# Batch 0 of a linear-attention and feed-forward kernel: k, v, q loaded in this order as fp32, q taken in pieces of tokens

## The chip, the cores and the metric

The kernel runs on one core of one Trainium2 chip. TensorE (PE) multiplies matrices, VectorE (DVE) and ScalarE (ACT) do elementwise work and read PE's results out of PSUM, GpSimd (POOL) and SyncE (SP) mostly issue DMAs here. Each engine takes its instructions in program order and waits for others by semaphores. The metric is the device time in microseconds. A profile is of one execution, with its span and the names of the engines as above; "PEld" is PE's weight load.

## The reference

```python
def phi(x):
    return np.where(x > 0, x, np.exp(x) - 1.0) + 1.0
q_p, k_p = phi(q), phi(k)                      # q, k, v: (8, 8, 576, 64) fp32
kv  = np.einsum('bhsd,bhse->bhde', k_p, v)
z   = np.sum(k_p, axis=2)
num = np.einsum('bhsd,bhde->bhse', q_p, kv)
den = np.einsum('bhsd,bhd->bhs', q_p, z)[..., None] + 1e-06
x   = (num / den).transpose(0, 2, 1, 3).reshape(8 * 576, 512)
h   = x @ w_in                                 # (512, 2048)
g   = h * (1.0 / (1.0 + np.exp(-beta * h)))
out = g @ w_out                                # (2048, 512)
```

The kernel computes phi as min(exp(x), max(x, 0) + 1), and g as Silu(beta * h) with 1/beta put into w_out.

## The kernel before, in words

A batch has 576 tokens; a token is 9 g + j, with g from 0 to 63 on partitions and j from 0 to 8 in the free dimension (J = 9). Eight heads lie as two "pr" (pairs of pairs), two "i" or "il" and two halves of the partitions, "a" or "hh". Blocks of two j make four token blocks t = 0 to 3 of 128 rows, and j = 8 is a tail block t = 4 of 64 rows, which is kept in xT_tail and multiplied at the very end for all batches together.

A batch goes through: loads of q, k, v; phi (phi_exp on ACT, line 161, phi_relu and phi_min on DVE, lines 166 and 174); transposes of phi(q) on PE; kv and z; numerators and denominators; xs = numerator times 1/denominator (bf16); transposes of xs into xT; h_mm (line 398), the product with w_in, in 16 chunks ff; silu (line 411), ACT's evacuation into g; y_mm (line 416) or y_fast, the product with w_out. The attention part of batch b+1 is put among the y products of batch b. The order is written by hand: the kernel asks for a manual schedule, so the order of the source lines is that of each engine's queue.

The front is lines 106 to 617, batch 0, in which no earlier products lie beside the attention:

- Loads (lines 106 to 138). SyncE's queue takes q in two halves of heads (x0f[0], x0f[1]) and k in two (x0f[2], x0f[3]), all fp32, into the buffer "stage" and the memory of xk[0]. POOL's queue waits by a small copy, "gate" (line 123), for q's first half and then issues v in two halves, cast to bf16 by the DMA (v0b, in vf's memory), w_in in four quarters (cast as well), w_out's first two quarters in fp32 (into the memory of g of batch 1), and q and k of batch 1 (cast). load_w_out(2) and load_w_out(3) go into stage, load_v(1) into vf as fp32; these and load_qk(2) are issued at lines 620 to 623.
- PE begins with 11 products on made-up data (idle, line 151), and more of them fill waits.
- phi of q's first half, its transposes (q_half, line 243), the same for the second half, q_last for the tail; phi of k's halves.
- z is computed by itself (z_sums, 18 products of one column per half), kv_first (line 511) makes kv from 128-column products that hold two heads and their cross terms, kv_mask and zbd remove the cross terms by a mask on DVE. All denominators come from 20 products into one bank, dps, and denom (line 557).
- numer_first(t) (line 565) makes the numerators of block t on PE and xs on DVE; x_first(t) transposes them and copies to xT; h_first(t) makes 16 products of 128 columns, the part of h chunks ff = 0 to 3 that belongs to block t. silu of these four banks needs all four blocks. Chunks 4 to 15 follow as 512-column products.

Y0, lines 632 to 698, holds batch 0's y products with batch 1's attention among them: y_mm(0, t, i) adds w_out's quarter i to token block t, four products of 512 columns each; kv_both(1) (line 213) uses vaug, v of batch 1 with a column of ones, which ACT and POOL cast from vf (lines 650 and 651). w_out_scale (line 449) makes w_out's quarters from their fp32 loads. The pool of PSUM banks for kv, numerators and x transposes has two buffers there (line 619).

Of the kernel before, what the change touches and what calls it, by code (L numbers as in the profile page):

```python
# [16 lines left out]
def kernel(  # L17
# [65 lines left out]
    x3f = xk[0].rearrange("p i j d -> p (i j d)").bitcast(F32)  # L83
    x0f = [
        a.rearrange("p (i j d) -> p i j d", i=2, j=J)
        for a in [stage[:, n * 1152 : (n + 1) * 1152] for n in range(3)] + [x3f]
    ]
# [52 lines left out]
    kvmask = consts.tile([P, 2, 2, EA], BF16)  # L140
    nc.vector.memset(kvmask, 0.0)
    nc.vector.memset(kvmask[:D, :, 0, :], 1.0)
    nc.vector.memset(kvmask[D:P, :, 1, :], 1.0)
    ones = consts.tile([P, 1], BF16)
    nc.vector.memset(ones, 1.0)
# [333 lines left out]
    qtp = [bank1("qtp", [P, 1024], BF16) for _ in range(2)]  # L479
    phi_part(0, "q", 0)  # L480
    q_half(0, 0, qtp[0])
    idle(3)
    phi_part(0, "q", 1)
    q_half(0, 1, qtp[1])
    t8 = bank1("qtp8", [P, 2 * P], BF16)
    q_last(0, t8)
    bps = bank("bps", [P, FC])
    nc.tensor.matmul(bps, beta_row, ident16, is_transpose=True, start=True, stop=True)
    idle(4)
    x = xin(0, "k", 0)  # L490
    phi_exp(0, "k", 0, x)
    phi_relu(0, "k", 0, x)
    q_copy(nc.vector, 0, 0, qtp[0])
    phi_min(0, "k", 0)


    zps = [bank("zps") for _ in range(2)]
    zbd = consts.tile([P, 2, 2, 2], BF16)

    def z_sums(pr):  # L500
        for j in range(J):
            for hh in range(2):
                nc.tensor.matmul(
                    zps[hh][:, pr : pr + 1], st[0, "k"][half(hh), pr, j, :], ones[half(hh)],
                    start=(j == 0), stop=(j == J - 1), skip_group_check=True,
                )

    kvp0 = [bank1("kvp0") for _ in range(2)]
    kv0 = consts.tile([P, 2, 2, 2 * D], BF16)

    def kv_first(pr):
        for j in range(J):
            for hh in range(2):
                nc.tensor.matmul(
                    kvp0[hh][:, pr * P : (pr + 1) * P],
                    st[0, "k"][half(hh), pr, j, :],
                    v0b[half(hh), 2 * pr : 2 * pr + 2, j, :],
                    start=(j == 0), stop=(j == J - 1), skip_group_check=True,
                )

    def kv_mask(pr):
        for hh in range(2):
            nc.vector.tensor_mul(
                kv0[:, hh, pr].rearrange("p (h d) -> p h d", h=2),
                kvp0[hh][:, pr * P : (pr + 1) * P].rearrange("p (h d) -> p h d", h=2),
                kvmask[:, hh, :, 0:D],
            )

    z_sums(0)
    idle(1)  # L530
    phi_part(0, "k", 1)
    q_copy(nc.scalar, 0, 1, qtp[1])
    q_copy_last(nc.scalar, 0, t8)
    nc.scalar.copy(beta_s, bps)
    table(ACTF.Silu)
    kv_first(0)
    z_sums(1)
    idle(1)
    kv_mask(0)
    for hh in range(2):  # L540
        nc.vector.tensor_mul(
            zbd[:, hh], zps[hh][:, 0:2, None].to_broadcast([P, 2, 2]), kvmask[:, :, :, 0]
        )
# [11 lines left out]
    dv = dps.rearrange("p t a b c -> p t (a b c)")

    def denom(r, ts):
        nc.vector.tensor_scalar(den0[:r, ts], dv[:r, ts], 1e-6, None, ALU.add)
        nc.vector.reciprocal(rden0[:r, ts], den0[:r, ts])

    kv_first(1)
    denom(P, slice(0, NT - 1))
    kv_mask(1)

    def numer_first(t):
        n = rows_of(t)
        nps = bank1("nps0", [P, 2, 2, P])
        for hh in range(2):
            for pr in range(2):
                nc.tensor.matmul(  # L570
                    nps[:n, hh, pr], st[0, "qT"][:, pr, t, hh, 0:n], kv0[:, hh, pr, :],
                    start=True, stop=True, skip_group_check=True,
                )
        nc.vector.tensor_mul(
            xs_tile(0, t),
            nps[:n].rearrange("p a b (c d) -> p a (b c) d", d=D),
            rden0[:n, t].rearrange("p (a i) -> p a i", a=2)[:, :, :, None].to_broadcast(
                [n, 2, 4, D]
            ),
        )  # L580

    def x_first(t, eng):
        x_trans(0, t, eng, bank1("xtp0", [P, KC, P], BF16))


    hp0 = []

# [15 lines left out]
    h_first(1)
    x_first(3, nc.scalar)
    nc.vector.tensor_mul(beta_m, beta_s, beta_s)
    nc.vector.tensor_scalar(beta_m, beta_m, TINY * TINY, 2.0 * TINY, ALU.is_lt, ALU.mult)
    nc.vector.tensor_add(beta_c, beta_s, beta_m)
    nc.vector.reciprocal(rbeta, beta_c)
    h_first(2)
# [303 lines left out]
```

## Time and profile before

| | |
|---|---|
| Median of 3 runs | 278.42 us (278.10 to 278.65) |
| The profiled execution | 277.78 us, span 276.0 us |
| PE busy | 267.8 us (97% of the span) |
| DVE, ACT busy | 169.7 us (61%), 170.1 us (62%) |
| DMA moved | 42.76 MB, mean 155 GB/s |
| First h product of batch 0 | 16.67 us after the span's start |
| Last of the four h_first starts | 20.55 us |
| First h product of batch 1 | 51.09 us |

The profile's times are counted from the span's start. Lines of the timeline give start, duration, engine, source line, operation, output <- inputs, shapes and count; in brackets stands the idle time before and what ended it. A helper's line stands for all its callers (L404 is every h product). Busy time by stretch gives, for PE, PEld, DVE, ACT and POOL, the busy us and the count, then PE's granted clock, the DMA share and the GB/s moved.

### The profile page before, as it was taken

What the parts mean: (1) busy time and instruction counts of PE and PEld (TensorE: products, weight loads), DVE (VectorE), ACT (ScalarE), POOL (GpSimd) and SP (SyncE); (2) the same over time, 40 slices, a digit from 0 to 9 for tenths busy, and PEclk for the clock granted to TensorE, in tenths of its full rate; (3) what the DMA queues carried; (4) which work ended last, traced back from release to release, by engine and by line L of the source; (5) the groups of instructions that cost most, each with busy time, mean ns of one, the idle gap of its engine ahead of it and who ended that gap; (6) DMA issues with size and microseconds to landing.
All of it is one profiled execution on the core that took longest, in us unless ns stands there. A gap on an engine that the chain in (4) does not pass through costs nothing.

```text
span 276.0 us, 6367 instructions
## 1 busy us (share of the span) xinstructions
PE 267.8 (97%) x2688; PEld 167.6 (61%) x2697; DVE 169.7 (61%) x329; ACT 170.1 (62%) x232; POOL 45.6 (17%) x60
## 2 busy tenths in 40 slices
PE   7899999999999999999999999999999999999994
PEld 2575455444445487548754885488548845874683
DVE  4771585967956997568857884779473414342532
ACT  4838887966915794579457945794573077117610
POOL 5922011042123040303030403040000000000000
PEclk9999999999999999999999999999999999999999
DMA  6999999569969946996799659956531040022013
GB/s 231 254 206 352 255 387 250 177 109 192 297 109 189 312 65 109 196 289 78 102 201 289 81 89 209 296 79 88 154 66 22 13 141 0 0 68 87 0 40 114
DMA packets 49228, 42.76 MB, mean 155 GB/s; under 512 B 30752, under 2 KB 41008, under 8 KB 49200
## 3 DMA queue, kind: packets, MB, share of 16 engines
q0 software_dynamic: 13040, 23.40, 36.4%
q1 hardware_dynamic: 35984, 18.82, 32.3%
q8 instruction: 21, 0.34, 0.5%
q10 hardware_dynamic: 176, 0.14, 0.2%
q14 instruction: 7, 0.06, 0.1%
HBM read 36.71 MB, written 9.44 MB: 167 GB/s over the span
## 4 chain that ended last, share of the span: by engine, by line
PE 82%; DMA 13%; DVE 1%; POOL 1%; issue 1%; ACT 0%; DVEq 0%; POOLq 0%
PE h_ps L404 41%; PE yb L795 9%; PE ya L795 9%; PE yd L795 9%; DMA vf<-in_v_dram 8%; PE y_ps L419 6%; PE yc L795 4%; DMA w_in<-in_moe_w_in_dram 4%; PE kvp L223 2%; PE nps L331 2%; DMA stage<-in_q_dram 1%; POOL vf L100 1%; PE nps L298 1%; DVE xs_sb L311 1%; ACT vaug L239 0%
## 5 line engine op out<-in xcount | busy, mean ns | idle before, releaser
L412 ACT ACTIVATE g<-h_ps,beta_c 128x512 bf16<-128x512 f32 x144 | 97.8, 688 | 69.1 <-PE h_ps L404 69.1
L404 PE MATMUL h_ps<-xT,w_in 128*128 128x512 bf16 (+1 forms) x560 | 114.5, 361 | 0.1
L404 PEld LDWEIGHTS <-w_in 128*128 128x128 bf16 x624 | 57.4, 98 | 62.3 <-issue 0.2
L795 PEld LDWEIGHTS <-stage 128*128 128x128 bf16 x448 | 43.8, 98 | 5.2
L795 PEld LDWEIGHTS <-g 128*128 128x128 bf16 x336 | 32.9, 98 | 5.3
L241 POOL CAST vaug<-vf 128x1152 bf16<-128x1152 f32 x13 | 18.4, 1443 | 74.7 <-DMA vf<-in_v_dram 74.7
L419 PE MATMUL y_ps<-w_out,g 128*128 128x512 bf16 x122 | 28.4, 379 | 0.4 <-issue 0.2
L795 PE MATMUL ya<-w_out,g 128*128 128x256 bf16 x224 | 26.7, 273 | 0.0
L725 DVE TENSOR_TENSOR stage<-g 128x1024 bf16<-128x1024 bf16 x14 | 9.6, 686 | 22.8 <-ACT g L412 22.8
L729 DVE TENSOR_TENSOR stage<-g 128x1024 bf16<-128x1024 bf16 x14 | 9.7, 691 | 19.2 <-ACT g L412 19.2
L346 DVE TENSOR_TENSOR xs_sb<-nps,rden 128x448 bf16<-128x448 f32 (+3 forms) x30 | 20.7, 689 | 1.0
L419 PEld LDWEIGHTS <-g 128*128 128x128 bf16 x128 | 12.2, 98 | 13.5
L163 ACT ACTIVATE e<-xk 128x1152 bf16<-128x1152 bf16 (+1 forms) x15 | 16.7, 1159 | 0.3 <-DMA xk<-in_k_dram 0.3
L163 ACT ACTIVATE e<-xq 128x1152 bf16<-128x1152 bf16 x14 | 15.6, 1160 | 0.0
L175 DVE TENSOR_TENSOR phi_k<-e,r 128x1152 bf16<-128x1152 bf16 x16 | 13.5, 850 | 1.4
L156 ACT ACT_TABLE_LOAD x11 | 14.1, 1283 | 0.2
L404 PE MATMUL h_ps<-xT_tail,w_in 128*128 128x512 bf16 x62 | 13.9, 379 | 0.1
L795 PE MATMUL yd<-ws,stage 128*128 128x256 bf16 x112 | 13.4, 273 | 0.0
L795 PE MATMUL yb<-ws,stage 128*128 128x256 bf16 x112 | 13.4, 272 | 0.0
L795 PE MATMUL yc<-ws,stage 128*128 128x256 bf16 x112 | 13.4, 273 | 0.0
L795 PE MATMUL yd<-ws,g 128*128 128x256 bf16 x112 | 13.4, 273 | 0.0
L795 PE MATMUL yb<-w_out,stage 128*128 128x256 bf16 x112 | 13.4, 272 | 0.0
(98 smaller groups left out, 233.8 us busy)
## 6 DMA issues: line engine op xcount, KB each, us to landing
vf<-in_v_dram POOLq DMA_DIRECT2D x7, 1152.0 KB, 13.3
out_dram<-y SPq DMA_DIRECT2D x25, 256.0 KB, 3.8
xq<-in_q_dram POOLq DMA_DIRECT2D x7, 576.0 KB, 8.3
xk<-in_k_dram POOLq DMA_DIRECT2D x7, 576.0 KB, 10.9
out_dram<-y SPq DMA_DIRECT2D x17, 128.0 KB, 2.9
w_in<-in_moe_w_in_dram POOLq DMA_DIRECT2D x4, 512.0 KB, 11.8
g<-in_moe_w_out_dram POOLq DMA_DIRECT2D x2, 1024.0 KB, 17.4
stage<-in_moe_w_out_dram POOLq DMA_DIRECT2D x2, 1024.0 KB, 21.6
```

The costliest lines, as they stand in the source:

```text
L156: nc.scalar.activation(act0, warm[:, 0:1], func)
L163: nc.scalar.activation(e, x, ACTF.Exp)
L175: nc.vector.tensor_tensor(st[b, a][:, pr].rearrange("p j (h d) -> p j h d", h=2), st[b, a, pr, "e"].rearrange("p h j d -> p j h d"), st[b, ...
L223: nc.tensor.matmul(t[half(il), a, pr * EA : (pr + 1) * EA], st[b, "k"][half(a), pr, j, il * D : (il + 1) * D], vaug[b % 2][half(a), pr, j, ...
L241: eng.tensor_copy(dst, src)
L346: nc.vector.tensor_mul(xs_sb[:n, ils, v0 * D : v1 * D].rearrange("p i (u d) -> p i u d", d=D), pv[:, :, :, 0:D], rden[:, :, :, None].to_br ...
L404: nc.tensor.matmul(hp[:, c0:c1].rearrange("p (t n) -> p t n", n=P), w_in_sb[ff // 4][:, kc, (ff % 4) * P : (ff % 4 + 1) * P], xm, start=(k ...
L412: nc.scalar.activation(g_sb[b % 2][:, ff, :], hp, ACTF.Silu, scale=beta_c[:, ff : ff + 1])
L419: nc.tensor.matmul(yp[:, c0:c1], g_sb[b % 2][:, ff, t * P : (t + 1) * P], w_out_sb[i][:, c, c0:c1], start=(ff == 0), stop=(ff == FC - 1), ...
L725: nc.vector.tensor_sub(gs[2][:, c], g[:, c, 0:HM], g[:, c, HM:512])
L729: nc.vector.tensor_add(gs[0][:, c], g[:, c, HM:512], g[:, c2, HM:512])
L795: nc.tensor.matmul(ps[:, p * HM : (p + 1) * HM], lhs(c, p), rhs(c), start=(first and (p == 0 or apart) and c == 0), stop=True, skip_group_ ...
```

## The change

Batch 0's loads on SyncE's queue become k in two halves, v in two halves (fp32, into vf) and q in two pieces of tokens: all heads with j = 0 to 3 (four j, blocks 0 and 1), then j = 4 to 8. POOL's gate waits for k's second half, and its queue no longer loads v. v is cast on chip into vaug, the first half by ACT, the second by DVE (v_copy). kv and the sums of phi(k) come from the same products by vaug's column of ones, in 64x65 products as in kv_both; kv_out copies them from PSUM into kv_bd, two copies per pr and half, and the mask, the ones and z_sums are gone. phi of q is done by pieces (class Part): j 0-1 and j 2-3 for all heads, then j 4-8 for each pr. q_first(t) transposes one block. Blocks 0 and 1 go through denominator, numerator, xs, x transposes and h_first before blocks 2, 3 and 4 are transposed. beta's sums are moved ahead on DVE. load_w_out(3) becomes two DMAs of half the size, and in Y0 kv_both(1) stands one y_mm later, with numer(1, 0) and numer(1, 1) directly behind each other.

```diff
-    load(nc.sync, x0f[0], q, 0, 0, 2)
-    load(nc.sync, x0f[1], q, 0, 2, 2)
-    load(nc.sync, x0f[2], k, 0, 0, 2)
-    load(nc.sync, x0f[3], k, 0, 2, 2)
+    for pr in range(2):
+        load(nc.sync, x0k[pr], k, 0, 2 * pr, 2)
+    for pr in range(2):
+        load(nc.sync, vf[:, 2 * pr : 2 * pr + 2], v, 0, 2 * pr, 2)
+    load(nc.sync, x0q[0], q, 0, 0, 4, 0, 4)
+    load(nc.sync, x0q[1], q, 0, 0, 4, 4, 5)
...
-    nc.gpsimd.tensor_copy(gate, x0f[0][:, 1, J - 1, D - 1 : D])
-    load(nc.gpsimd, v0b[:, 0:2], v, 0, 0, 2)
-    load(nc.gpsimd, v0b[:, 2:4], v, 0, 2, 2)
+    nc.gpsimd.tensor_copy(gate, x0k[1][:, 1, J - 1, D - 1 : D])
...
+    bps = bank("bps", [P, FC])
+    nc.tensor.matmul(bps, beta_row, ident16, is_transpose=True, start=True, stop=True)
+    idle(6)
...
+    for pr in range(2):
+        phi_part(0, "k", pr)
+    nc.vector.tensor_copy(beta_s, bps)
+    nc.vector.tensor_mul(beta_m, beta_s, beta_s)
+    nc.vector.tensor_scalar(beta_m, beta_m, TINY * TINY, 2.0 * TINY, ALU.is_lt, ALU.mult)
+    nc.vector.tensor_add(beta_c, beta_s, beta_m)
+    nc.vector.reciprocal(rbeta, beta_c)
...
     def kv_first(pr):
         for j in range(J):
+            for il in range(2):
+                for a in range(2):
+                    nc.tensor.matmul(
+                        kvp0[a][half(il), pr * EA : (pr + 1) * EA],
+                        st[0, "k"][half(a), pr, j, il * D : (il + 1) * D],
+                        vaug[0][half(a), pr, j, il, 0:EA],
+                        start=(j == 0), stop=(j == J - 1), skip_group_check=True,
+                    )
+
+    def kv_out(pr, a, eng):
+        for il in range(2):
+            copy(
+                eng, kv_bd[half(il), a, pr, il], kvp0[a][half(il), pr * EA : (pr + 1) * EA]
+            )
+
+    class Part:
...
+        def exp(self):
+            nc.scalar.activation(self.e, self.x, ACTF.Exp)
+
+        def relu(self):
+            nc.vector.tensor_scalar(self.r, self.x, 0.0, 1.0, ALU.max, ALU.add)
+
+        def min(self):
+            for i in range(0, self.n, 2):
+                nc.vector.tensor_tensor(
...
+    def q_first(t, eng):
+        tp = bank1("qtp", [P, 512], BF16)
+        for pr in range(2):
+            for jj in range(2):
                 nc.tensor.matmul(
+                    tp.rearrange("p (r h i g) -> p r h i g", r=2, h=2, i=2)[:, pr, :, jj, :],
+                    st[0, "q"][:, pr, 2 * t + jj, :], identity,
+                    is_transpose=True, start=True, stop=True, skip_group_check=True,
...
+    v_copy(nc.scalar, 0, 0)
+    kv_first(0)
+    v_copy(nc.vector, 0, 1)
+    for a in range(2):
+        kv_out(0, a, nc.vector)
+    idle(2)
+    kv_first(1)
+    idle(3)
+    qa = [Part(x0q[0][:, :, 2 * n : 2 * n + 2], 0, 2 * n) for n in range(2)]
+    for n in range(2):
+        qa[n].exp()
+        qa[n].relu()
+        if n == 0:
+            qa[0].min()
+    kv_out(1, 0, nc.vector)
+    kv_out(1, 1, nc.scalar)
+    q_first(0, nc.scalar)
+    qa[1].min()
+    den_mm(dps, (0,))
+    numer_mm0(0)
+    denom(dps, P, slice(0, 1))
+    numer_xs0(0)
+    q_first(1, nc.scalar)
+    dps1 = bank("dps", dps_shape)
+    den_mm(dps1, (1,))
+    numer_mm0(1)
+    qb = [Part(x0q[1][:, 2 * pr : 2 * pr + 2], 2 * pr, 4) for pr in range(2)]
+    qb[0].exp()
     x_first(0, nc.scalar)
+    denom(dps1, P, slice(1, 2))
+    numer_xs0(1)
     h_first(0)
+    qb[0].relu()
+    qb[0].min()
+    qb[1].exp()
+    qb[1].relu()
+    table(ACTF.Silu)
+    x_first(1, nc.vector)
+    qb[1].min()
+    h_first(1)
+    q_first(2, nc.scalar)
+    q_first(3, nc.vector)
+    t8 = bank1("qtp8", [P, 2 * P], BF16)
+    q_last(0, t8)
+    q_copy_last(nc.vector, 0, t8)
+    dps = bank1("dps", dps_shape)
+    den_mm(dps, (2, 3, 4))
+    numer_mm0(2)
+    numer_mm0(3)
+    denom(dps, P, slice(2, 4))
+    numer_xs0(2)
+    numer_xs0(3)
+    denom(dps, G, slice(4, 5))
     x_first(2, nc.scalar)
+    h_first(2)
+    numer_mm0(4)
+    numer_xs0(4)
     x_first(3, nc.scalar)
+    h_first(3)
     x_first(4, nc.vector)
...
-    load_w_out(3)
+    load_w_out(3, 2)
...
-    for t in range(2):
+    for t in range(3):
         y_mm(0, t, 2, yps[t])
     kv_both(1)
...
-    y_mm(0, 2, 2, yps[2])
+    y_mm(0, 3, 2, yps[3])
     numer(1, 0)
-    y_mm(0, 3, 2, yps[3])
     numer(1, 1)
+    y_mm(0, 0, 3, yps[0])
     x_trans(1, 0, nc.scalar)
...
-    y_mm(0, 0, 3, yps[0])
     numer(1, 2)
```

numer_mm0(t) makes block t's four numerator products, numer_xs0(t) its xs on DVE, den_mm its four denominator products, denom adds 1e-6 and takes reciprocals.

More of the change, by code (lines that the diff above doesn't have):

```diff
@@ L82 @@
     ]
[L83 to L86, printed above, removed]
-    ]
-    v0b = vf.rearrange("p i j d -> p (i j d)").bitcast(BF16)[:, 0:2304].rearrange(
-        "p (i j d) -> p i j d", i=4, j=J
-    )
+    x0k = [
+        stage[:, n * 1152 : (n + 1) * 1152].rearrange("p (i j d) -> p i j d", i=2, j=J)
+        for n in range(2)
+    ]
+    x0q = [
+        xk[0].rearrange("p i j d -> p (i j d)").bitcast(F32)[:, 0:1024].rearrange(
+            "p (i j d) -> p i j d", i=4, j=4
+        ),
+        stage[:, 2304:3584].rearrange("p (i j d) -> p i j d", i=4, j=5),
+    ]
     st_b = stage.bitcast(BF16)
@@ L96, with load @@
     ws = [consts.tile([P, 8, HM], BF16, name=f"ws{i}") for i in range(4)] if FAST else None
-    def load(eng, dst, src, b, i0=0, n=4):
+    def load(eng, dst, src, b, i0=0, n=4, j0=0, nj=J):
         return eng.dma_start(
             out=dst.rearrange("p i j d -> p i (j d)"),
-            in_=src[b].rearrange("(i a) (g j) d -> (a g) i (j d)", a=2, j=J)[:, i0 : i0 + n],
+            in_=src[b].rearrange("(i a) (g j) d -> (a g) i (j d)", a=2, j=J)[
+                :, i0 : i0 + n, j0 * D : (j0 + nj) * D
+            ],
         )
@@ L130, with load_w_out @@
         nc.gpsimd.dma_start(out=w_in_sb[i], in_=w_in_v[:, :, i * 512 : (i + 1) * 512])
-    def load_w_out(i):
-        nc.gpsimd.dma_start(out=w_out_f[i], in_=w_out_v[:, i * 4 : (i + 1) * 4, :])
+    def load_w_out(i, n=4):
+        for c in range(0, 4, n):
+            nc.gpsimd.dma_start(
+                out=w_out_f[i][:, c : c + n], in_=w_out_v[:, i * 4 + c : i * 4 + c + n, :]
+            )
     load_w_out(0)
@@ L138 @@
     load(nc.gpsimd, xk[1], k, 1)
[L140 to L145, printed above, removed]
     for i in range(2):
@@ L183, in xin @@
         if b == 0:
-            return x0f[pr if a == "q" else 2 + pr]
+            return x0k[pr]
         return (xk if a == "k" else xq)[b % 2][:, 2 * pr : 2 * pr + 2]
@@ L478 @@
     q_tile(0)
[L479 to L506, printed above, removed]
+    for pr in range(2):
+        phi_part(0, "k", pr)
+    nc.vector.tensor_copy(beta_s, bps)
@@ L508 @@
+    nc.vector.tensor_mul(beta_m, beta_s, beta_s)
+    nc.vector.tensor_scalar(beta_m, beta_m, TINY * TINY, 2.0 * TINY, ALU.is_lt, ALU.mult)
+    nc.vector.tensor_add(beta_c, beta_s, beta_m)
+    nc.vector.reciprocal(rbeta, beta_c)
     kvp0 = [bank1("kvp0") for _ in range(2)]
-    kv0 = consts.tile([P, 2, 2, 2 * D], BF16)
     def kv_first(pr):
         for j in range(J):
-            for hh in range(2):
+            for il in range(2):
[6 more added lines that the diff above has]
+                    )
@@ new lines, in kv_out, with __init__ @@
+    def kv_out(pr, a, eng):
+        for il in range(2):
+            copy(
+                eng, kv_bd[half(il), a, pr, il], kvp0[a][half(il), pr * EA : (pr + 1) * EA]
+            )
+    class Part:
+        def __init__(self, x, i0, j0):
+            self.x, self.i0, self.j0 = x, i0, j0
+            self.n, self.nj = x.shape[1], x.shape[2]
+            self.e, self.r = [
+                work.tile([P, 2, J, D], BF16, tag=s, name=s, bufs=4).rearrange(
+                    "p i j d -> p (i j d)"
+                )[:, 0 : self.n * self.nj * D].rearrange("p (i j d) -> p i j d", i=self.n, d=D)
+                for s in ("e", "r")
+            ]
+        def exp(self):
[5 more added lines that the diff above has]
+                nc.vector.tensor_tensor(
+                    st[0, "q"][:, (self.i0 + i) // 2, self.j0 : self.j0 + self.nj].rearrange(
+                        "p j (h d) -> p j h d", h=2
+                    ),
+                    self.e[:, i : i + 2].rearrange("p h j d -> p j h d"),
+                    self.r[:, i : i + 2].rearrange("p h j d -> p j h d"),
+                    ALU.min,
+                )
@@ L514, in kv_first @@
+    def q_first(t, eng):
+        tp = bank1("qtp", [P, 512], BF16)
+        for pr in range(2):
+            for jj in range(2):
                 nc.tensor.matmul(
[L515 to L518, printed above, removed]
-                )
[L521 to L542, printed above, removed]
+                    tp.rearrange("p (r h i g) -> p r h i g", r=2, h=2, i=2)[:, pr, :, jj, :],
+                    st[0, "q"][:, pr, 2 * t + jj, :], identity,
@@ L543, with den_mm @@
+                    is_transpose=True, start=True, stop=True, skip_group_check=True,
+                )
+        copy(
+            eng, st[0, "qT"][:, :, t].rearrange("p r h n -> p r (h n)"),
+            tp.rearrange("p (r x) -> p r x", r=2),
         )
-    dps = bank("dps", [P, NT, 2, 2, 2])
     den0 = consts.tile([P, NT, 8], F32)
     rden0 = consts.tile([P, NT, 8], F32)
-    for t in range(NT):
+    def den_mm(dps, ts):
+        for t in ts:
+            n = rows_of(t)
+            for hh in range(2):
+                for pr in range(2):
+                    nc.tensor.matmul(
+                        dps[:n, t, hh, pr], st[0, "qT"][:, pr, t, hh, 0:n],
+                        kv_bd[:, hh, pr, :, D], start=True, stop=True, skip_group_check=True,
+                    )
@@ L548, with denom, numer_mm0 @@
+    def denom(dps, r, ts):
+        dv = dps.rearrange("p t a b c -> p t (a b c)")
+        nc.vector.tensor_scalar(den0[:r, ts], dv[:r, ts], 1e-6, None, ALU.add)
+        nc.vector.reciprocal(rden0[:r, ts], den0[:r, ts])
+    def numer_mm0(t):
         n = rows_of(t)
+        nps = st[0, "nps", t] = bank1("nps0", [P, 2, 2, P])
         for hh in range(2):
@@ L551, with numer_xs0 @@
                 nc.tensor.matmul(
-                    dps[:n, t, hh, pr], st[0, "qT"][:, pr, t, hh, 0:n], zbd[:, hh, pr, :],
+                    nps[:n, hh, pr].rearrange("p (h d) -> p h d", h=2),
+                    st[0, "qT"][:, pr, t, hh, 0:n], kv_bd[:, hh, pr, :, 0:D],
                     start=True, stop=True, skip_group_check=True,
                 )
[L555 to L565, printed above, removed]
-        n = rows_of(t)
[L567 to L573, printed above, removed]
+    def numer_xs0(t):
+        n = rows_of(t)
         nc.vector.tensor_mul(
             xs_tile(0, t),
-            nps[:n].rearrange("p a b (c d) -> p a (b c) d", d=D),
+            st[0, "nps", t][:n].rearrange("p a b (c d) -> p a (b c) d", d=D),
             rden0[:n, t].rearrange("p (a i) -> p a i", a=2)[:, :, :, None].to_broadcast(
@@ L592, in h_first @@
             h_mm(xT[0], ff, hp0[ff], t * P, (t + 1) * P)
-    for t in range(3):
-        numer_first(t)
-    denom(G, slice(NT - 1, NT))
+    dps_shape = [P, NT, 2, 2, 2]
+    dps = bank("dps", dps_shape)
+    v_copy(nc.scalar, 0, 0)
[26 more added lines that the diff above has]
+    qb[0].exp()
     x_first(0, nc.scalar)
-    numer_first(3)
-    x_first(1, nc.scalar)
+    denom(dps1, P, slice(1, 2))
+    numer_xs0(1)
     h_first(0)
-    numer_first(4)
+    qb[0].relu()
[19 more added lines that the diff above has]
+    denom(dps, G, slice(4, 5))
     x_first(2, nc.scalar)
-    h_first(1)
+    h_first(2)
+    numer_mm0(4)
+    numer_xs0(4)
     x_first(3, nc.scalar)
[L605 to L609, printed above, removed]
+    h_first(3)
     x_first(4, nc.vector)
-    h_first(3)
     for ff in range(4):
```

## The prediction

> **What bounds the kernel now.** I read the page first, then the chain of waits, then the timeline of the first 21 us, the busy time by microsecond, and the waits. The page and the chain:
>
> ```profile
> span 276.0 us, 6367 instructions
> PE 267.8 (97%) x2688; PEld 167.6 (61%) x2697; DVE 169.7 (61%) x329; ACT 170.1 (62%) x232; POOL 45.6 (17%) x60
> PE 82%; DMA 13%; DVE 1%; POOL 1%; issue 1%; ACT 0%; DVEq 0%; POOLq 0%
> ```
>
> TensorE (PE) is the bound. From the first product of batch 0 to the end it hardly rests, so a change in the front counts in full by the time at which that stream starts, unless the stream later waits for something else and returns the time. The timeline shows the start:
>
> ```profile
> 4.45 1.16 ACT L163 ACTIVATE e<-stage 128x1152 bf16<-128x1152 f32 x1 [1.74 <-DMA stage<-in_q_dram]
> 9.58 1.16 ACT L163 ACTIVATE e<-xk 128x1152 bf16<-128x1152 f32 x1 [0.28 <-DMA xk<-in_k_dram]
> 11.34 0.68 PE L514 MATMUL kvp<-vf,phi_k 64*128 64x128 bf16 x18 [0.65 <-DMA vf<-in_v_dram]
> 14.85 1.29 DVE L574 TENSOR_TENSOR xs_sb<-nps,rden 128x512 bf16<-128x512 f32 x2 [0.31 <-PE nps L570]
> 16.67 1.05 PE L404 MATMUL h_ps<-xT,w_in 128*128 128x128 bf16 x16
> 18.23 1.06 PE L404 MATMUL h_ps<-xT,w_in 128*128 128x128 bf16 x16
> 18.43 0.59 ACT L239 COPY xT<-xtp 128x512 bf16<-128x512 bf16 x1 [1.21 <-PE xtp L386]
> 19.35 1.06 PE L404 MATMUL h_ps<-xT,w_in 128*128 128x128 bf16 x16
> 20.55 11.43 PE L404 MATMUL h_ps<-xT,w_in 128*128 128x128 bf16 x64
> ```
>
> The four x16 or x64 rows are h_first(0) to h_first(3). They start at 16.67, 18.23, 19.35 and 20.55, and all of xT is there by the last, after which PE goes on without a gap. It can go so closely because every phi, q transpose and denominator was done before: when v's second half is in (kv_first(1) at 13.35), only numerators, evacuations and transposes are left, and VectorE (DVE) makes one xs every 0.65 us.
>
> The second place is Y0, where the next batch's v is awaited:
>
> ```profile
> 40.62 1.15 ACT L239 CAST vaug<-vf 128x1152 bf16<-128x1152 f32 x1 [1.06 <-DMA vf<-in_v_dram]
> 41.83 0.80 PE L223 MATMUL kvp<-vaug,phi_k 64*64 64x65 bf16 x72 [0.21 <-ACT vaug L239]
> 49.55 0.23 PEld L386 LDWEIGHTS <-xs_sb 128*128 128x128 bf16 x4 [0.63 <-DVE xs_sb L311]
> ```
>
> PE's idle time from 40 to 50 us, by microsecond, is 0.03, 0.23, 0.16, 0.09, 0, 0.13, 0, 0.03, 0, 0.19: 0.86 us, about 0.25 of it the wait for v. That is all that the Y0 half of the change can win. The DMA rate while SyncE's queue alone moves fp32:
>
> ```profile
> 3.00:4.00 1.00, 1.00 (x4) 0.31 (x3) 0.00 (x0) 0.00 (x0) 0.00 (x0) 1.00 1.03 399
> 4.00:5.00 1.00, 1.00 (x4) 0.45 (x3) 0.55 (x1) 0.55 (x1) 0.52 (x1) 1.00 1.07 401
> 13.00:14.00 1.00, 1.00 (x32) 0.86 (x29) 0.51 (x2) 0.50 (x2) 0.75 (x1) 1.00 1.24 208
> ```
>
> The last column is GB/s written: 400 for fp32, 208 where the load casts (two bytes read for one written). So bytes read go at some 400 GB/s either way, and casting v on chip changes nothing in the total.
>
> **Landings.** A 590 KB piece takes 1.47 us at 400 GB/s. SyncE's four pieces were used at 4.45, 6.37, 8.13 and 9.58; these places now hold k, k, v, v. POOL's gate waits for the second landing, not the first, so its first load (now w_in) is issued at about 6.8 to 7.2 (landing plus 0.78 for the gate), against 5.19 for v and 6.74 for w_in before. Without v's cast load beside them, places 2 to 4 land at 5.9, 7.4 and 8.9 at the earliest and as before at the latest; I take 5.95, 7.4, 9.2. The q pieces (524 and 655 KB, 1.31 and 1.64 us alone) land at 10.2 and 11.8 if w_in leaves them alone, at 12.2 and 14.5 if it halves their rate from 9 us on. I take 10.9 and 13.2, nearer the first, since in 6 to 9 us the rows at 359, 408 and 341 GB/s written say that SyncE's queue kept most of the rate. w_in's first quarter landed 8.5 us after its issue at 6.74; now it has no v ahead of it, so 15.2 at the latest, before it is needed. The rest of POOL's loads come after the same bytes as before; w_out's last quarter in two halves costs one more issue (0.75 us) on a queue that has room.
>
> **The new front, engine by engine in program order.** Durations: ACT 1.16 us for 1152 columns, 0.59 for 512 from PSUM, so 0.63 and 0.74 estimated for exp of 512 and 640; DVE min 0.76 for 1152, estimated 0.27 to 0.30 for 256 and 0.48 for 640; relu fp32 0.75, estimated 0.42 and 0.48; kv_out of 64x65 estimated 0.23 (64x260 takes 0.43, 128x8 0.17); four transposes or four numerator products 0.40 with the next ones after 0.23; xs 0.65; denominator 0.17 + 0.20; xT copy 0.59 on ACT, 0.41 on DVE; h_first 1.05, 0.9 to the next. A hop between engines takes 0.05.
>
> To 11.1: k's phi ends at 8.1 on DVE; the five beta instructions, 0.95 with their 0.16 to 0.25 rows, run to 9.2 and hide behind v's landing. ACT casts v's first half 7.45 to 8.6 (1.15), DVE the second 9.25 to 10.05 (estimated 0.8, as a 1152 relu). Four kv_out on DVE: 11.1. The removed z sums, masks and ones lie before this and are worth nothing by themselves. kv is ready some 2 us earlier than before, but q now comes last.
>
> To 16.4: DVE does relu, two mins, relu, two kv_out, two mins of q's first piece: 0.42 + 0.57 + 0.42 + 0.5 + 0.57 with gaps, to 13.8. PE has transposed block 0 (12.65), ACT's copy waits behind exp and two kv_out and ends at 13.4, den and numerator 13.4 to 14.0, denominator to 14.2, xs(0) to 14.9. ACT has copied block 1's q and started exp of the second q piece; PE transposes x at 15.3 to 15.7, ACT copies to 16.3, h_first(0) at 16.4. Before: 16.67. Behind ACT's exp here stands xT's copy, so a late q piece delays h_first(0) too.
>
> To 19.3: DVE finishes xs(1) at 16.3 and does relu, min, relu of the second piece to 17.9, then xT's copy of block 1 to 18.3 and the last min to 18.8. h_first(1) at 18.35, issued by 19.25. Before: 18.23.
>
> To 25.9: only now come blocks 2 to 4, and nothing lies beside them. q transposes (two sets of four and a tail) to 19.9, copies on ACT 20.3 and DVE 20.35 and 20.65, twelve den products and eight numerators 20.7 to 21.75, denominator to 21.8, xs(2) to 22.5, x transposes 22.95, ACT copy 23.6, h_first(2) 23.65 to 24.55, then numerator 4 and x transposes of block 3 (25.15), whose ACT copy ends at 25.8. h_first(3) starts at 25.9 against 20.55: +5.3 us. Block 4's transposes, 0.23 of issue, stood ahead of h_first(3) and now follow it: +0.2.
>
> The Exp-to-Silu table load (1.28) stays beside PE's h_first(0), behind the last exp; ACT's next copy is at 19.7, so it costs nothing until that exp is a microsecond later.
>
> [...] The row first: 11 warm-up products took 4.87 us (0.44 each), three at 7.29 took 0.86 with the latency of the last. [...]
>
> **Y0.** With PE 5.5 us later, v (40.6) and w_out's last quarter (43.2) have landed before they are needed: kv_both would come at 47.9, ACT's cast of v at 45.2 to 46.3 behind exp. The 0.25 wait goes. Next late is the rest: one y_mm (0.86) fewer lies behind kv_both, and numer(1,0) and numer(1,1) follow each other, so that numer(1,2) waits for the bank that xs(1,1) frees. DVE needs 1.1 us per tile (0.18 + 0.20 + 0.69), two are 2.2; PE has y_mm and two short sets between, 1.5. Up to 0.7 lost there, up to 0.86 won in all: between -0.7 and +0.6; I take 0, the ends being equally near.
>
> **Sum.** 5.3 + 0.2 + 0 = +5.5. The profiled execution took 277.78 (span 276.0 and 1.78 around it): 283.3. The median of the runs is 0.64 above it: 283.9.
>
> **The rivals.** (1) Late q: w_in halves the q loads' rate, pieces at 12.2 and 14.5. For: 210 and 190 GB/s in 5 to 6 and 9 to 10 us, where POOL's casts had the engines. Against: 341 to 408 between. h_first(3) at 27.6, +7.2: 285.6. (2) PE cools in the sparse stretch from 10 to 25 us, where about half of it is busy, and the first products go at the 0.44 of the warm-up. Against: PE was warm at 16.67 after gaps up to 0.65. The first warm-up lasted from 1.46 to about 7, so half of 5.5 us is the bound, +2.7: 286.6. (3) The small instructions cost a tenth less, kv_out 0.17, pieces at 10.2 and 12.3: h_first(3) at 24.3, +3.9: 282.3. (4) Not slower: phi of q's second piece is done so early that blocks 2 to 4 follow h_first(1) without a break. The chain from that last min to h_first(3) is 6.5 us of the steps above, so it decides if the min ends by 14.0 rather than 18.8. For: that piece can land at 11.8. Against: DVE and ACT work in order, with 5 us of other work ahead of it. With the min at 13.7 h_first(3) starts at 20.2; with Y0's wait gone (-0.25) and +0.2: 278.0.
>
> **How the numbers follow.** My forecast 0.60 (283.9, own range 282.6 to 285.3), rival 1 0.13, rival 2 0.11, rival 3 0.07, rival 4 0.09. Below 281.0 lies rival 4; above 287.0 half of rival 2 and what it adds to rival 1, 0.07. A measurement can tell 0.2% (0.56 us) from no change. Of rival 4 I give 0.07 to faster and 0.02 to same; the rest, 0.91, is slower.
>
> **What would show it.** h_first(0) to (3) at about 16.4, 18.4, 23.6 and 25.9, with PE idle between 19.5 and 25.9 on "DVE xs_sb" and ACT's copies; the last min of q near 18.8; no DMA wait ahead of kv_both in Y0; from there the two timelines some 5.5 us apart to the end. It is wrong if h_first(2) follows h_first(1) within 2 us, or if the h products after 26 us are spaced 0.43 rather than 0.22.

## The result and the profile after

The changed kernel takes 289.84 us (288.84 to 290.56, 4 runs) against 278.26 us (277.96 to 278.65, 4 runs): a ratio of 1.0413 with a 95% interval of 1.0374 to 1.0452, or 11.6 us more. The sign of the prediction was right, its size (283.9) and its range (281.0 to 287.0) were not. Beside the last four experiments the kernel before itself took 279.31 us, at a mean clock of 0.988 and on average 1.6 us more in four of its eight runs, so those four are read against each other and by their timelines.

The page of the changed kernel; in its second row each digit is the clock that PE was granted in a fortieth of the span, in tenths:

```profile
span 288.8 us, 6393 instructions
PE 274.3 (95%) x2690; PEld 171.8 (59%) x2699; DVE 170.9 (59%) x339; ACT 171.8 (59%) x236; POOL 43.0 (15%) x59
PEclk9975699999999999999999999999999999999999
```

The row of the kernel before held nothing but nines. Here the clock is down in the third to fifth fortieth, 14 to 36 us. The timeline shows the four h_first and the first 512-column products:

```profile
17.52 1.87 PE L406 MATMUL h_ps<-xT,w_in 128*128 128x128 bf16 x16 [0.76 <-ACT xT L241]
20.33 1.87 PE L406 MATMUL h_ps<-xT,w_in 128*128 128x128 bf16 x16 [0.51 <-DVE xT L243]
26.77 1.86 PE L406 MATMUL h_ps<-xT,w_in 128*128 128x128 bf16 x16 [0.67 <-ACT xT L241]
30.42 1.87 PE L406 MATMUL h_ps<-xT,w_in 128*128 128x128 bf16 x16 [0.67 <-ACT xT L241]
32.55 11.44 PE L406 MATMUL h_ps<-xT,w_in 128*128 128x512 bf16 x48
```

Two things are to be seen. The four no longer follow each other: 17.5, 20.3, 26.8 and 30.4 us in place of 16.7, 18.2, 19.35 and 20.55. And each takes 1.87 us in place of 1.05. Busy time in stretches of 3.4 us (span of the stretch, then PE, PEld, DVE, ACT and POOL busy, granted clock, DMA share, GB/s) shows since when:

```profile
6.90:10.30 3.40, 1.70 (x42) 0.89 (x40) 1.80 (x8) 1.32 (x2) 3.40 (x6) 1.00 1.01 353
10.30:13.70 3.40, 1.89 (x58) 1.13 (x45) 3.21 (x9) 1.57 (x4) 2.25 (x3) 1.00 1.16 280
13.70:17.10 3.40, 1.71 (x29) 1.24 (x27) 2.77 (x11) 2.01 (x4) 0.55 (x1) 1.00 1.23 213
17.10:20.50 3.40, 2.46 (x23) 2.30 (x22) 2.36 (x6) 2.50 (x4) 0.97 (x2) 0.54 1.25 206
20.50:23.90 3.40, 3.36 (x37) 3.00 (x36) 0.80 (x3) 0.59 (x1) 0.71 (x1) 0.50 1.15 309
23.90:27.30 3.40, 2.34 (x22) 1.90 (x22) 1.98 (x6) 0.59 (x1) 1.36 (x2) 0.50 1.03 391
30.70:34.10 3.40, 3.40 (x23) 2.14 (x22) 1.45 (x5) 2.42 (x4) 0.00 (x0) 0.50 1.19 263
34.10:37.50 3.40, 3.40 (x16) 1.52 (x15) 3.40 (x10) 2.45 (x4) 0.00 (x0) 0.95 1.04 404
```

For three stretches PE is busy about half of the time, then the clock falls to 0.50 (at 17.34 us) and stays there until 34.41 us, although PE is busy for 3.36 of 3.40 us from 20.50 us on. In the kernel before the same three stretches from 6.9 us hold 3.11, 2.64 and 2.77 us of PE. The other three runs of the changed kernel have a mean clock of 0.968, 0.976 and 0.981 where this one has 0.970: by an estimate from these and the spans, the half rate lasted from 11 to 18 us in the four.

Where the time went, by places in the two timelines (us from the span's start, and differences):

| place | before | after | grown by |
|---|---|---|---|
| h_first(0) | 16.67 | 17.52 | 0.85 |
| batch 0's first y product | 31.82 | 43.82 | 11.15 more |
| batch 1's first h product | 51.09 | 63.61 | 0.52 more |
| end of the span | 276.0 | 288.8 | 0.28 more |

So all but 0.8 us is there when batch 0's h products are done. Theory A: the half rate costs some 5 us of it, the serial chain of q's last blocks the rest. Theory B: late landings and the chain alone make it and the fallen clock costs nothing on the path.

### The profile page after: what moved, and what is told of

It reads as the page before. It is cut to its first block, busy times and chain, and to the rows that moved or that the text cites. A ratio compares the mean times of both kernels' runs of the same rounds, so it can differ in the third digit from the quotient of the medians.

```text
span 288.8 us, 6393 instructions
## 1 busy us (share of the span) xinstructions
PE 274.3 (95%) x2690; PEld 171.8 (59%) x2699; DVE 170.9 (59%) x339; ACT 171.8 (59%) x236; POOL 43.0 (15%) x59
## 4 chain that ended last, share of the span: by engine, by line
PE 87%; DMA 4%; DVE 3%; ACT 2%; issue 1%; SPq 1%; ACTq 0%; DVEq 0%
PE h_ps L406 45%; PE y_ps L421 9%; PE yd L849 8%; PE yb L849 8%; PE ya L849 7%; DMA stage<-in_q_dram 4%; PE yc L849 4%; PE kvp L225 2%; PE nps L333 2%; PE xtp L388 1%; SPq L103 1%; ACT e L165 1%; DVE phi_q L177 1%; ACT xT L241 1%; DVE xs_sb L313 0%
## 5 line engine op out<-in xcount | busy, mean ns | idle before, releaser
L406 PE MATMUL h_ps<-xT,w_in 128*128 128x512 bf16 (+1 forms) x560 | 118.8, 373 | 2.6 <-ACT xT L241 2.1
L406 PEld LDWEIGHTS <-w_in 128*128 128x128 bf16 x624 | 60.8, 103 | 66.1 <-issue 4.5
L243 POOL CAST vaug<-vf 128x1152 bf16<-128x1152 f32 x13 | 17.5, 1373 | 78.6 <-DMA vf<-in_v_dram 78.6
L177 DVE TENSOR_TENSOR phi_q<-e,r 128x1152 bf16<-128x1152 bf16 x14 | 13.0, 926 | 12.1 <-ACT e L165 11.0
L165 ACT ACTIVATE e<-xk 128x1152 bf16<-128x1152 bf16 x14 | 15.5, 1159 | 0.0
```

Of the source, the lines that this page charges most:

```text
L165: nc.scalar.activation(e, x, ACTF.Exp)
L177: nc.vector.tensor_tensor(st[b, a][:, pr].rearrange("p j (h d) -> p j h d", h=2), st[b, a, pr, "e"].rearrange("p h j d -> p j h d"), st[b, ...
L243: eng.tensor_copy(dst, src)
L406: nc.tensor.matmul(hp[:, c0:c1].rearrange("p (t n) -> p t n", n=P), w_in_sb[ff // 4][:, kc, (ff % 4) * P : (ff % 4 + 1) * P], xm, start=(k ...
```

## The experiments

**Filling PE's waits.** e1 adds 19 made-up products of 512 columns in the waits up to h_first(0) (6, 5, 2, 3 and 3; its expectation says 16), e2 also 35 short ones between h_first(0) and h_first(3).

```diff
 e1 (and e2)
-    idle(6)
+    idle(12)
...
-    idle(2)
+    idle(7)
     kv_first(1)
     idle(3)
...
     q_first(0, nc.scalar)
+    idle(2)
...
     q_first(1, nc.scalar)
+    idle(3)
...
     x_first(0, nc.scalar)
+    idle(3)
 e2 besides, fill(n, c0) being n products into hp0[3][:, c0:512]
     x_first(1, nc.vector)
+    fill(5, 256)
...
     q_copy_last(nc.vector, 0, t8)
+    fill(6, 256)
...
     numer_mm0(3)
+    fill(9, 256)
...
     x_first(2, nc.scalar)
+    fill(5, 256)
     h_first(2)
...
     x_first(3, nc.scalar)
+    fill(10, 384)
     h_first(3)
```

> The changed kernel with 16 more made-up products of 512 columns in PE's waits from 8 to 17 us, up to h_first(0), and none later. Theory A (PE's half rate from about 17.3 to 34.2 us costs some 5 us, and it is the thin work of the 8 to 17 us before that brings it): the clock is still full at h_first(0) and h_first(1), which end 0.8 us sooner each; the second thin stretch, 20 to 26 us, may then bring the fall later, so between 284.5 (no fall) and 289 us. Theory B (late landings of v and q and the serial chain alone make the loss, the clock falls with no cost on the path): 289.8, within 0.6.

> As the run before, and with 35 more short made-up products (128 or 256 columns, into columns of the last h bank that are not written yet) in PE's waits between h_first(0) and h_first(3). Theory A: granted clock 1.00 throughout, the four h_first at about 17.5, 19.6, 25 and 27 instead of 17.5, 20.3, 26.8 and 30.4 us, and 284.5 us (from 284 to 285.5): 3.3 us saved on the four h_first, 1.0 on the first 512-column products, about 1 on transposes and small products. Theory B: 289.8 or, by the added products, up to 1 us more.

Measured: e1 284.69 us (ratio 1.0223, 1.0188 to 1.0258), e2 284.42 (1.0222, 1.0197 to 1.0248). Work was added and 5.2 to 5.4 us went away. The timeline of e1:

```profile
17.13 1.05 PE L406 MATMUL h_ps<-xT,w_in 128*128 128x128 bf16 x16
19.00 1.05 PE L406 MATMUL h_ps<-xT,w_in 128*128 128x128 bf16 x16 [0.59 <-DVE xT L243]
23.96 1.05 PE L406 MATMUL h_ps<-xT,w_in 128*128 128x128 bf16 x16 [0.67 <-ACT xT L241]
26.36 1.05 PE L406 MATMUL h_ps<-xT,w_in 128*128 128x128 bf16 x16 [0.67 <-ACT xT L241]
27.57 6.65 PE L406 MATMUL h_ps<-xT,w_in 128*128 128x512 bf16 x30
```

h_first takes 1.05 us again and the four come at 17.1, 19.0, 24.0 and 26.4. Theory B has fallen: the half rate costs 5.2 to 5.4 us by the medians, and the work that is thin before 17 us decides, since e2's later fillers add nothing to e1's. (Two of e1's four executions took 283.6 and 284.1 us at a mean clock of 1.000 and 0.999, the other two 285.3 us at 0.993; against the first two the half rate costs 6 us.) The chain remains: from h_first(0) to h_first(3) 9.2 us against 3.9 in the kernel before.

**Which thin stretch.** e11 has only the fillers from 8 to 12 us, e12 only those from 14 to 17 us.

```diff
 e11
-    idle(6)
+    idle(12)
...
-    idle(2)
+    idle(7)
     kv_first(1)
 e12
     q_first(0, nc.scalar)
+    idle(2)
...
     q_first(1, nc.scalar)
+    idle(3)
...
     x_first(0, nc.scalar)
+    idle(3)
```

> The changed kernel with made-up products added only in PE's waits from 8 to 12 us (6 + 5), none from 14 to 17. The clock fell at 17.0 us, after 3.4 us (13.8 to 17.2) with PE busy 1.61 of 3.4. If that stretch alone brings the fall, it falls all the same: 289 to 290. If the thin work before it counts as well: 284.5 to 285.5.

> The changed kernel with made-up products added only in PE's waits from 14 to 17 us (2 + 3 + 3), none earlier. If the stretch from 13.8 to 17.2 alone brings the fall: full clock, 284.6, from 284 to 285.5. If the thin work from 8 to 13 us counts as well (1.70 of 3.4 and 1.99 of 3.5): a fall in some runs, 285.5 to 290.

Measured: e11 286.64 us, e12 286.69 us; neither is as slow as the changed kernel or as quick as e1. Busy time around the fall of e11, then of e12:

```profile
13.40:16.90 3.50, 1.76 (x29) 1.30 (x28) 2.98 (x11) 2.15 (x4) 0.59 (x1) 0.98 1.24 209
16.90:20.00 3.10, 2.29 (x21) 2.13 (x20) 2.15 (x6) 2.36 (x4) 0.92 (x2) 0.50 1.24 205
20.00:23.50 3.50, 3.46 (x35) 3.10 (x35) 0.97 (x3) 0.58 (x1) 0.70 (x1) 0.50 1.18 291
23.50:24.00 0.50, 0.50 (x10) 0.48 (x10) 0.17 (x1) 0.00 (x0) 0.44 (x1) 0.89 0.99 410
```

```profile
9.40:12.90 3.50, 1.34 (x70) 0.97 (x73) 2.48 (x6) 1.63 (x3) 3.13 (x5) 0.99 1.12 310
12.90:16.40 3.50, 3.50 (x43) 1.87 (x32) 2.25 (x10) 1.10 (x4) 0.00 (x0) 0.52 1.24 218
16.40:17.00 0.60, 0.55 (x6) 0.24 (x4) 0.51 (x1) 0.36 (x1) 0.39 (x1) 1.00 1.19 196
```

In e11 the clock falls to 0.50 at 16.79 us after 3.5 us with PE busy for half of them, in e12 at 12.82 after 3.5 us with PE busy for 38%. In both it returns after 3.5 us in which PE hardly rested (3.46 and 3.50 us busy). So both thin stretches matter: in these two executions, with only one of them filled, the fall came at the other. The fall of e12 is over at 16.23 us, but the small products and fillers within it took longer (four q transposes 0.63 us instead of 0.41, two fillers 1.06 instead of 0.59), so h_first(0) comes at 18.69 instead of e1's 17.13; the later fall of e11 takes h_first(0) and (1) with it (1.87 and 1.86 us instead of 1.05). The expectation that e11 falls to the changed kernel's time was wrong by some 3 us: the clock was back at 23.61 rather than 34.41 us. e4 below, whose front is that of the changed kernel, shows yet another place: in its profiled execution (287.62 us, mean clock 0.974) four q transposes at 13.86 us already took 0.63 us, h_first(0) and (1) 1.87 each, and h_first(2), at 27.79, 1.05 again.

**The same fillers taken from the kernel before.**

```diff
     q_half(0, 0, qtp[0])
-    idle(3)
...
-    idle(4)
     x = xin(0, "k", 0)
...
     z_sums(0)
-    idle(1)
...
     z_sums(1)
-    idle(1)
```

> The kernel before without the nine made-up products that stand in PE's waits from 7 to 13 us (3 + 4 + 1 + 1; the first eleven stay). If thin work on PE for some 3 us is enough to bring the half rate, and these fillers are what keeps the kernel before from it, the clock falls before or within the four h_first and the time is 281 to 284 us. If the work that is left is dense enough, or the fillers' place is not what matters, 278.3 within 0.6.

Measured: 279.92 us, ratio 1.0052 (1.0026 to 1.0077). Its busy time:

```profile
4.60:8.10 3.50, 1.61 (x13) 0.65 (x10) 2.66 (x4) 2.11 (x2) 3.50 (x5) 1.00 0.98 337
8.10:15.00 6.90, 5.17 (x104) 4.60 (x105) 4.89 (x12) 5.06 (x7) 5.58 (x7) 0.50 1.20 220
15.00:18.50 3.50, 3.34 (x32) 2.98 (x32) 3.06 (x8) 0.95 (x2) 0.92 (x2) 0.52 1.24 208
18.50:19.50 1.00, 1.00 (x18) 0.81 (x15) 0.13 (x1) 0.23 (x1) 0.59 (x1) 1.00 1.23 201
```

The clock falls here too, to 0.50 for 10.24 us, and the loss is 1.5 us, less than expected. h_first(0) comes at 17.93 instead of 16.67 us, so most of the loss is there by then. In the kernel before PE is busy for 8.56 of the same 10.24 us, made-up products among them, so part of the slower work fits into its waits. 10.24 us at the half rate cost 1.5 us here, 17.07 us cost 5.2 to 5.4 in the changed kernel: the author's reading is that how much of PE's own work on the path lies within the fall sets the price.

**Q earlier.** e6 is e2 with POOL's gate on q's last piece, so that no w_in load runs beside batch 0's.

```diff
-    nc.gpsimd.tensor_copy(gate, x0k[1][:, 1, J - 1, D - 1 : D])
+    nc.gpsimd.tensor_copy(gate, x0q[1][:, 3, 4, D - 1 : D])
```

> The filled version of the changed kernel (284.4 us) with POOL's gate on the landing of q's last piece in place of k's second half, so that no w_in load shares the DMA engines with batch 0's fp32 loads. If the late landings (v 8.6 and 10.2, q 11.7 and 16.2 us) carry the loss: q's last piece lands near 12 us, h_first(0) comes near 16.3, h_first(3) 1 to 3 us sooner, 282 to 283.4 us. If the serial chain on DVE, ACT and PE carries it: at most 1.2 us sooner at h_first(0) by v, 283.3 to 284.4; w_in's first quarter then lands near 15.5 us.

Measured: 287.26 us, 2.8 us more than e2. The gate, the loads of w_in and h_first(0) and (3):

```profile
13.01 0.41 POOL L130 CAST gate<-stage 128x1 bf16<-128x1 f32 x1 [10.93 <-DMA stage<-in_q_dram]
13.36 3.12 POOL L135 DMA_DIRECT2D w_in<-in_moe_w_in_dram  x4
18.96 1.07 PE L406 MATMUL h_ps<-xT,w_in 128*128 128x128 bf16 x16 [2.00 <-DMA w_in<-in_moe_w_in_dram]
28.30 1.05 PE L406 MATMUL h_ps<-xT,w_in 128*128 128x128 bf16 x16
```

Q's last piece is there at 13.0 instead of 16.2 us, and from h_first(0) to h_first(3) it is still 9.3 us: q's landing is not what makes the chain long. The loss is another: w_in's first quarter landed 5.6 us after its issue, not some 2 us as expected, and PE waited for it.

**The order behind q's second piece.** e9 is e1 with Y0 as before; e10 is e9 with another order for blocks 1 to 4.

```diff
 e9: Y0's order and load_w_out(3) as in the kernel before
 e10 besides
-    h_first(1)
     q_first(2, nc.scalar)
     q_first(3, nc.vector)
...
     q_copy_last(nc.vector, 0, t8)
+    h_first(1)
...
     numer_xs0(2)
-    numer_xs0(3)
     denom(dps, G, slice(4, 5))
+    numer_xs0(3)
     x_first(2, nc.scalar)
-    h_first(2)
     numer_mm0(4)
     numer_xs0(4)
     x_first(3, nc.scalar)
+    h_first(2)
     h_first(3)
```

> The changed kernel with the 16 early made-up products (284.6 us) and Y0's order and w_out's last quarter as before. In every run so far the stretch from kv_both(1) to batch 1's first h product takes 9.2 us, with six y_mm behind kv_both or with five; so a y_mm moved ahead of kv_both would cost its own length, and taking it back saves 0.86: 283.7, from 283.2 to 284.2. If Y0's order costs only where v is awaited: 284.6.

> The run before with the order behind q's second piece changed: blocks 2 to 4 are transposed ahead of h_first(1), which then fills their copies' time, x of block 3 is transposed ahead of h_first(2), so that its copy lies beside that, and the tail's denominator comes ahead of xs(3). If what is left of the loss is the serial chain from q's last min to h_first(3), the first 512-column product comes 1.7 us sooner (25.9 instead of 27.6 us) and the time is 1.7 less, 282.0, from 281.5 to 282.7. If landings or the engines' load set it, within 0.5 of the run before.

Measured: e9 284.15 us, e10 281.88 us (281.75 to 282.18), 2.3 us less for the same work in another order. The timeline of e10:

```profile
20.05 1.06 PE L406 MATMUL h_ps<-xT,w_in 128*128 128x128 bf16 x16
23.95 1.95 PE L406 MATMUL h_ps<-xT,w_in 128*128 128x128 bf16 x32
26.06 8.16 PE L406 MATMUL h_ps<-xT,w_in 128*128 128x512 bf16 x37
```

The first 512-column product comes at 26.06 against 27.53 in e9 and 25.9 expected; h_first(2) and (3) are one row now. 1.5 us of the 2.3 are there; the two profiled executions differ by 1.9, and the rest is not located. The instructions are the same and v and q landed no sooner than in e9, so the order alone gave this back. That the rest of the 5.3 us by which the four h_first are drawn out comes from the same serial steps is read from the timelines and from e7 below; no run shows it by itself.

**One part of the change alone: v on chip.** e7 keeps q, k, v and whole halves of q, but takes v as fp32 by SyncE's queue, casts it on ACT and DVE and makes kv with the column of ones.

```diff
     load(nc.sync, x0f[3], k, 0, 2, 2)
+    for pr in range(2):
+        load(nc.sync, vf[:, 2 * pr : 2 * pr + 2], v, 0, 2 * pr, 2)
...
-    nc.gpsimd.tensor_copy(gate, x0f[0][:, 1, J - 1, D - 1 : D])
-    load(nc.gpsimd, v0b[:, 0:2], v, 0, 0, 2)
-    load(nc.gpsimd, v0b[:, 2:4], v, 0, 2, 2)
+    nc.gpsimd.tensor_copy(gate, x0f[2][:, 1, J - 1, D - 1 : D])
...
-    z_sums(0)
-    idle(1)
+    idle(6)
     phi_part(0, "k", 1)
+    v_copy(nc.scalar, 0, 0)
...
     kv_first(0)
-    z_sums(1)
-    idle(1)
-    kv_mask(0)
...
+    idle(6)
+    v_copy(nc.vector, 0, 1)
+    for a in range(2):
+        kv_out(0, a, nc.vector)
+    kv_first(1)
+    idle(2)
+    kv_out(1, 0, nc.vector)
+    kv_out(1, 1, nc.scalar)
```

> The kernel before with one part of the change: q, k, v in the old order and q by whole halves, but v as fp32 by SyncE's queue, cast on chip (ACT and DVE), kv and the sums of phi(k) from one run with the column of ones, no mask; 14 made-up products in PE's waits in place of the two that stood among the z sums. If q last and by pieces carries the remaining 6 us, this costs only the casts and kv_out ahead of the first xs (near 16.0 instead of 14.85 us) and follows with blocks 1 us apart as before: 279.4, from 278.5 to 280.2. If casting v on chip carries it, 282 or more.

Measured: 280.71 us, ratio 1.0083 (1.0054 to 1.0113), between the two expectations. Its h_first(0) and (3):

```profile
19.18 1.05 PE L395 MATMUL h_ps<-xT,w_in 128*128 128x128 bf16 x16
23.08 11.43 PE L395 MATMUL h_ps<-xT,w_in 128*128 128x128 bf16 x64
```

h_first(0) is 2.5 us later than in the kernel before, and the four take 3.9 us as there. v's halves were there at 11.11 and 12.58 us, no later than in the kernel before (11.34 and 13.03), so it is the casts, kv_out and the 20 denominator products that now stand behind it (0.95 us) that cost 2.3 us where v comes last. In the whole change loading k and v first hides most of that (h_first(0) 0.5 us late in e1). What it pays is the chain, q's phi and transposes after h_first(0): with q first the four follow within 3.9 us.

**Y0 alone, and undone.** e3 is the kernel before with the Y0 half of the change, e4 the changed kernel without it (both as in the diff of the change).

> The kernel before with only the Y0 half of the change: kv_both(1) one y_mm later, numer(1,0) and numer(1,1) directly after each other, w_out's last quarter in two DMAs. The prediction's step says 0 within -0.7 and +0.6: 278.3, from 277.6 to 278.9. If Y0 carries part of the loss by itself (the wait of numer(1,2) for a bank, 0.67 us in the changed kernel's timeline), 279 or more.

> The changed kernel with Y0's order and w_out's last quarter as before. If the Y0 half costs nothing, 289.8 within 0.6; if the banks' wait at numer(1,2) costs what its timeline shows and the old order has no wait for v any more with PE 12 us later, 0.5 to 0.9 less, 289.0.

Measured: e3 279.36 us, ratio 1.0045 (1.0020 to 1.0069): 1.1 us more. e4 289.56 us (287.62 to 290.97), which these runs cannot tell from 289.84. In e3 the kv products and batch 1's first h products, with numer(1,2) between:

```profile
42.55 0.80 PE L226 MATMUL kvp<-vaug,phi_k 64*64 64x65 bf16 x72
47.12 0.39 PE L301 MATMUL nps<-kv_bd,qT 128*128 128x130 bf16 x4 [0.67 <-ACT xT L242]
51.82 8.81 PE L407 MATMUL h_ps<-xT,w_in 128*128 128x512 bf16 x40
```

and in e9, with the old order and PE late enough not to wait for v:

```profile
47.63 0.80 PE L225 MATMUL kvp<-vaug,phi_k 64*64 64x65 bf16 x72
56.83 3.41 PE L406 MATMUL h_ps<-xT,w_in 128*128 128x512 bf16 x15
```

From kv_both to batch 1's h it is 9.27 us in e3, 9.20 in e9, 9.26 in the kernel before, 9.20 in the changed one: the same with five y_mm in between or with six. So a y_mm that is moved ahead of kv_both costs its own 0.86 us, unless PE would wait for v there. From batch 0's first y product to batch 1's first h the new order takes 19.79 us in e1 and the old one 18.93 in e9, 0.86 apart; the medians differ by 0.5.

**A gate that was to help the kernel before.** The kernel before with w_in held back until v's first half has landed:

```diff
     load(nc.gpsimd, v0b[:, 2:4], v, 0, 2, 2)
+    gate2 = consts.tile([P, 1], BF16)
+    nc.gpsimd.tensor_copy(gate2, v0b[:, 1, J - 1, D - 1 : D])
```

> The kernel before with a second wait of POOL, on v's first half, ahead of the w_in loads, so that v does not share the DMA engines with w_in. If the landing of v's second half (13.0 us) sets the front, it lands 1 to 1.5 us sooner, the four h_first follow as much sooner, and PE's later stalls in Y0 take some of it back because the DMA stream ends when it did: 277.3, from 276.8 to 278.2. If w_in's first quarter then comes too late, or Y0 takes all back, 278.3 or more.

Measured: 280.17 us, ratio 1.0061 (1.0038 to 1.0084); a miss. The issue, two microseconds of the DMA engines, and h_first(0):

```profile
11.79 2.98 POOL L132 DMA_DIRECT2D w_in<-in_moe_w_in_dram  x4
12.00:14.00 2.00, 1.97 (x58) 1.52 (x55) 1.15 (x6) 1.58 (x4) 2.00 (x3) 1.00 0.34 24
17.50 1.07 PE L406 MATMUL h_ps<-xT,w_in 128*128 128x128 bf16 x16 [0.96 <-DMA w_in<-in_moe_w_in_dram]
```

v's halves were used at 11.28 and 13.30, no sooner than in the kernel before, so w_in was not what delayed them. The DMA engines then stood nearly empty (24 GB/s) behind the late issue.

No version measured beats the kernel before. Two further versions of that kernel, one with more fillers in its front and one with a later exp in Y0 besides, were not measured.

## Why the prediction was wrong, point by point

- **The sum left out the clock.** The failed step is the half rate of PE, for which the sum (5.3 + 0.2 + 0) has no term and which is left to rival (2), "PE cools in the sparse stretch from 10 to 25 us", given 0.11 and a price of 2.7. The sign that the prediction named for it, h products 0.43 us apart after 26 us, is what came. The stretch was described rightly (about half busy), but the evidence set against it, a kernel before that stayed warm after gaps of 0.65 us, came from stretches with 78 to 91% of PE busy. The price took the first warm-up's 5.5 us as the bound of the half rate; it lasted 17 us in the profiled execution. In three of the five stretches of 3.41 us within it PE was busy for 2.35 to 2.75 us, and the clock stayed at 0.50; it came back after one with 3.41 us. But from 20.76 to 24.17 us PE was busy for 3.37 of 3.41 us, as long as in the stretch after which e11's clock returned, and here it did not; why is open. The fall cost 5.3 us: 0.82 on each of four h_first (3.3), and the first four or five 512-column products at 0.43 rather than 0.22 (about 1), with transposes and small products for the rest.
- **How thin the stretch was.** PE did not have to be wholly idle: the falls came with PE busy for 37 to 52% of the 3.41 us before them (1.26 us in e12, 1.79 in e11), and the longest, in the changed kernel, lasted 17.07 us.
- **The serial chain was right.** Predicted 16.4 to 25.9 us from h_first(0) to (3), 9.5 us; 9.2 in e1, 9.4 in e2, 9.3 in e6 with q 3 us earlier. e10 shows that the order makes at least 1.5 us of it.
- **The start of the chain was 0.7 to 1.1 us late.** v was cast from 8.73 and 10.21 us on, not 7.45 and 9.25, beyond the bound "as before at the latest" (8.13 and 9.58). In e6, with no w_in beside, it was cast from 8.26 and 9.77, in e1, with w_in beside, from 8.22 and 9.77, so these runs do not show that w_in makes it late. DVE's cast took 1.35 us, not 0.8: a relu of the same length was the wrong row for it.
- **Late q** (rival 1): it landed at 11.7 and 16.2, the second piece later than in the rival (14.5), and cost little: ACT waited 0.29 us for it.
- **Y0** was taken at 0 between -0.7 and +0.6 and cost 0.5 to 0.6 in the timelines of the changed kernel and of e3. numer(1, 2) waits there as forecast, 0.67 us; the profile names ACT's copy of xT as its end, which in the changed kernel ends 0.04 us after xs(1, 1), the step that the prediction named.
- **Together**, on e1's timeline: 0.46 us for the start, 5.35 for the chain, 0.31 from h_first(3) to the first y product (block 4) and 0.52 for Y0 make 6.64 at batch 1's first h product, and 6.4 are left at the end of the span. The changed kernel's span is 6.4 longer still, by the clock and by v, which was cast 0.44 later in that execution. Without the fall the forecast would have been 0.5 to 0.8 us too low (e2, e1).

## What to carry to other kernels

Before an order is changed at the front of a kernel that is bound by PE, add up PE's busy time over the stretches of the new order. In these runs the falls to the half rate came behind 3.41 us with 1.26 to 1.79 us of PE's work, though other stretches as thin brought none (1.61 us in the changed kernel, 1.80 in e12), and lasted 3.41 to 17.07 us. Where a new order is as thin, reckon with a fall, price it by all of PE's work on the path for as long, and put made-up products into the waits: in e1 19 of them took 5.2 us off. When the operand of the longest chain is loaded last, its blocks must be interleaved so that a copy of one lies beside the products of another; e10 got 2.3 us back by order alone. A y_mm moved from behind a chain of fixed length (9.2 us) to the front of it cost its full 0.86 us in the timelines of e1 and e9.

## What the runs showed of the hardware that was not expected

- The four falls whose start and end the busy times by 0.25 us show last 3.41 us (e12), 6.83 (e11), 10.24 (e5) and 17.07 (the changed kernel): one, two, three and five times 3.41. Why, no run shows.
- In the 3.41 us ahead of the fall PE was busy for 1.26 us (e12), 1.48 (the changed kernel), 1.51 (e5) and 1.79 (e11), 37 to 52%. Of the stretches of 3.41 us counted back from there, one with 1.61 us (47%, from 7.10 us on in the changed kernel) and one with 1.80 (53%, from 5.99 on in e12) brought no fall; nor did one not so counted that held 0.86 us (from 8.25 us on in the changed kernel). So the share of busy time alone does not decide.
- The clock returned after 3.25 us (e5), 3.37 (e11) and 3.41 (e12, the changed kernel) of busy time in 3.41. In the changed kernel it did not after 3.37 (20.76 to 24.17 us); why is open.
- The first of the four casting loads of w_in, 0.5 MB each, was used 5.6 us (e6) and 5.7 us (e8) after POOL issued it, though few other bytes moved: from 12 to 14 us 16 GB/s in e6, with the issue at 13.36, and 24 in e8, with the issue at 11.79; from 14 to 16 us 27 GB/s in e6.
- DVE's cast of 128x1152 fp32 into rows of 66 took 1.35 us, ACT's 1.15; DVE's relu of as many fp32 elements took 0.75 in the kernel before.
